# A new order of the pieces of a chunked gated-attention and MoE kernel, with the last stores split and on other queues

## The chip, the cores and the metric

The kernel runs on one core of one Trainium2 chip. The core has five engines that run side by side, each in the order of its own instruction stream: TensorE (PE in the profile; its weight loads are shown apart as PEld), VectorE (DVE), ScalarE (ACT), GpSimd (POOL) and SyncE (SP), which here only issues transfers. The metric is the device time of one execution in microseconds; less is better.

## The reference

There are two parts. The first is a gated linear attention over 4 batches, 8 heads, 768 positions and 48 dimensions; the second takes its output as a sequence of 384 features, makes a gate by a causal convolution of five taps, and multiplies by two matrices.

```python
f = 1.0 / (1.0 + np.exp(-f_logit))
for t in range(S):
    state = f[:, :, t, :, None] * state + np.einsum('bhd,bhe->bhde', k[:, :, t], v[:, :, t])
    y[:, :, t] = np.einsum('bhd,bhde->bhe', q[:, :, t], state)
...
x = y.transpose(0, 2, 1, 3).reshape(B, S, H * D)
for k in range(5):
    gate_pre += conv_w[k][None, None, :] * xp[:, k:k + S, :]
gate = 1.0 / (1.0 + np.exp(-gate_pre))
val = x @ w_val
return (gate * val @ w_out).astype(np.float32)
```

Here xp is x with four zero rows put in front.

## The kernel before

The sequence is cut into 6 chunks of 128 positions. Two heads lie together on the partitions, so a chunk has 16 pairs of batch and head pair. Inside a chunk the recurrence is turned into matrix products: with L the running sum of -log f, k is multiplied by exp(L) and q by exp(-L), so that scores are plain products of q and k, a triangular mask keeps the past, and the state is carried from chunk to chunk.

The work is cut into small pieces, each a function that emits a few instructions. PROGRAM is a text that lists all pieces in one order, written by a search outside of the kernel. The loop at line 762 emits them one by one, and the class Ordered ties every engine to exactly this order: each engine runs its own instructions as they come in PROGRAM, and waits where an input is not there yet. The first number of a piece is the chunk.

The attention's pieces, in the order in which a chunk needs them:

- loadf, loadk, loadq, loadv, loadw issue loads on SyncE. For chunk 0 the logits come from another layout, ft, in two parts (loadf 0 0 holds pairs 0 to 3, loadf 0 1 the rest); k, q and v of chunk 0 come in three parts (4, 4 and 8 pairs), those of later chunks in two halves.
- pexp and pln, on ScalarE: exp(-x), and then the log of 1 plus that, which is -log f. Then the running sum: by TensorE for chunk 0 (csum, into a pair of PSUM banks), by a VectorE scan for the others (scan).
- exp2 and exp1, on ScalarE: exp(L) and exp(-L). pmulk and pmulq, on VectorE: their products with k and q. okc notes on VectorE whether the numbers stay in range.
- ktrans (TensorE) and kevac (ScalarE): k transposed. dstate (TensorE), stend (VectorE) and stmul (GpSimd): the state of the next chunk.
- scores (TensorE, one per batch), mask (VectorE) and cross (ScalarE) bring the scores to SBUF; apply (TensorE, four per chunk) makes y, and xevac (ScalarE) copies it to XF. halo copies the last four columns of the chunk before.

The second part, for the same chunk: msplit (ScalarE) and mlow (VectorE) split x exactly in two parts; mlast (ScalarE) and mconv (VectorE, four taps by three groups m) do the convolution, for chunk 0 TensorE does it as one piece, conv; gate (ScalarE) is the sigmoid; mval (TensorE, nine matmuls) is x times w_val, mmul (VectorE) gates it, mhigh (ScalarE) and mrest (VectorE) split the result, mout (TensorE, nine matmuls) multiplies by w_out, mstore (ScalarE) copies it to SBUF and out issues the store. The last chunk is done as two halves of two batches, numbered 5 and 6.

weight n is one step of preparing a weight (n = 0 the convolution's taps, 1 to 3 w_val, 4 to 6 w_out): step 1 on GpSimd, 2 on ScalarE, 3 to 6 on VectorE, 7 on ScalarE and 8 on GpSimd (step 7, the last for n = 0, on GpSimd). wload n loads it.

busy n has n matmuls on a tile of zeros run in front of the next piece that takes a PSUM bank; they compute nothing.

What else sets the order. There are three pairs of PSUM banks and two single ones; a piece that takes a pair waits until the piece that frees it (cross, kevac, xevac, stend, exp1, gate) is through. Buffers of q, k, v and E1 are double, by chunk parity, E2 and vs are single. pace (line 662) lets the first 24 loads go as soon as SyncE reaches them and their buffer is free; each later load also waits for the last TensorE instruction that was emitted before it and for the fourth transfer before it:

```python
        if loads[0] > EAGER:
            for x in (PE.last, moves[-AHEAD]):
                tc.add_manual_dep(ins.ins, x.ins.name,
```

out n m takes SyncE's queue; with a third number 1 it takes ScalarE's. Stores up to chunk 4 leave from two buffers, osb, in turn; those of 5 and 6 from qb. When out 6 m is reached and out 5 m has not been, one transfer of 256 KB stores both halves:

```python
        if n == NC and (last, m) in bufs:
            bufs.pop((last, m))
            buf, dst = half(m, 0, 2), oview(last, m)
        moves.append((ACT if engine else SP).dma_start(dst, buf[:]))
```

In the profile nearly every instruction has line 128, the helper's; pieces are told apart by engine, tile and shape (asb for mask and cross, qb and kb on VectorE for pmulq and pmulk, work for the weights' steps, e on ScalarE for exp and log, banks<-xf,WD for conv).

Of the kernel before, what the change touches and what calls it, by code (L numbers as in the profile page):

```python
# [829 lines left out]
```

## Time and profile before

| What | us |
|---|---|
| median of 3 executions (lowest, highest) | 194.49 (192.51, 194.89) |
| the profiled execution's own time | 194.6 |
| its span, first to last instruction | 192.9 |
| TensorE busy | 176.0 |
| VectorE busy | 165.9 |
| ScalarE busy | 151.2 |
| GpSimd busy | 39.8 |
| last matmul over, last store issued | 187.4, 187.8 |

The profile is one execution taken by the hardware profiler. Busy is the time in which an engine worked on an instruction; a busy TensorE may still be at half clock, so the granted clock is read beside it (1.00 is full). Its mean over the span is 0.963. The groups of instructions give a count, the busy time, the mean of one in ns, and the idle time just before them with what ended it. Loads move 39 MB, at 205 GB/s over the span, and at up to 418 GB/s in the first 25 us.

### The profile page before, as it was taken

The numbers are of one execution on the slowest core, as the hardware profiler recorded it, in microseconds if no ns is written. First come the engines' busy times: TensorE is split into PE (matmuls) and PEld (weight loads), VectorE is DVE, ScalarE is ACT, GpSimd is POOL, SyncE is SP. The second block draws the span as 40 slices with busy tenths as digits, with TensorE's granted clock in tenths as the row PEclk, the third lists the DMA queues.
The fourth block names the chain that finished last, engine by engine and source line by source line (L and its number), as shares of the span: only waits on it lengthen the run. The fifth ranks groups of instructions, "written<-read, shape, count | busy, mean of one in ns | idle before, by whom it ended". The sixth has DMA issues, their size and how long they took to land.

```text
span 192.9 us, 7550 instructions
## 1 busy us (share of the span) xinstructions
PE 176.0 (91%) x3356; PEld 143.2 (74%) x3357; DVE 165.9 (86%) x235; ACT 151.2 (78%) x241; POOL 39.8 (21%) x43
## 2 busy tenths in 40 slices
PE   7869689995999989989999997999999999999980
PEld 2467577864788867878988796888887878898880
DVE  2528989899897999999899998998999999999710
ACT  5369949699469886998999999949897964986950
POOL 5110198076900682000600000000411000000000
PEclk9969969997599999999999999999999999999999
DMA  5999992993897599795389797003850020100161
GB/s 171 336 377 416 415 370 49 352 343 133 237 411 245 138 247 388 272 355 177 120 242 373 226 398 311 7 7 70 297 187 0 7 107 5 58 3 0 54 241 40
DMA packets 11989, 39.47 MB, mean 205 GB/s; under 512 B 1456, under 2 KB 2096, under 8 KB 11312
## 3 DMA queue, kind: packets, MB, share of 16 engines
q1 hardware_dynamic: 10800, 37.38, 54.9%
q10 hardware_dynamic: 1152, 1.57, 2.2%
q8 instruction: 27, 0.44, 0.9%
q14 instruction: 10, 0.08, 0.1%
HBM read 34.23 MB, written 4.72 MB: 202 GB/s over the span
## 4 chain that ended last, share of the span: by engine, by line
PE 75%; DVE 9%; ACT 5%; issue 4%; DMA 3%; SPq 1%; DVEq 0%
PE banks L128 75%; DVE work L128 4%; DMA e<-in_ft 3%; ACT e L128 3%; DVE qb L128 2%; ACT ksb L128 1%; DVE asb L128 1%; SPq L128 1%; DVE okc L128 1%; DVE xL L128 1%; DVE st L128 0%; DVE gt L128 0%; ACT asb L128 0%; ACT work L128 0%; ACT qb L128 0%
## 5 line engine op out<-in xcount | busy, mean ns | idle before, releaser
L128 ACT ACTIVATE e<-e 112x1024 f32<-112x1024 f32 (+3 forms) x36 | 44.4, 1239 | 4.8 <-DMA e<-in_ft 4.1
L128 DVE SCALAR_TENSOR_TENSOR pre<-xf,cws,pre 128x512 f32<-128x512 f32 x48 | 34.3, 749 | 0.9 <-ACT pre L128 0.8
L128 PE MATMUL banks<-rg,woH 128*128 128x512 f32 (+1 forms) x108 | 32.0, 381 | 0.0
L128 PE MATMUL banks<-qb,kb 48*64 48x128 f32 (+1 forms) x768 | 26.3, 266 | 5.3 <-DVE qb L128 2.5
L128 PE MATMUL banks<-asb,vb 128*32 128x64 f32 (+2 forms) x1152 | 29.2, 252 | 0.0
L128 PEld LDWEIGHTS banks<-qb,kb 48*64 48x64 f32 x768 | 22.3, 139 | 8.8 <-DVE qb L128 3.3
L128 POOL TENSOR_TENSOR st<-st,e 112x512 f32<-112x512 f32 x8 | 14.5, 1818 | 57.4 <-issue 30.1
L128 DVE TENSOR_TENSOR_SCAN e<-keep,e 112x1024 f32<-112x1024 bf16 x10 | 24.7, 2481 | 0.0
L128 PEld LDWEIGHTS banks<-asb,vb 128*32 128x32 f32 (+1 forms) x1152 | 23.6, 112 | 1.2 <-issue 0.9
L128 PEld LDWEIGHTS banks<-rg,woH 128*128 128x128 f32 x108 | 19.2, 188 | 4.1 <-issue 0.2
L128 PE MATMUL banks<-rg,woL 128*128 128x512 f32 (+1 forms) x54 | 20.3, 375 | 0.0
L128 PE MATMUL banks<-xH,wvH 128*128 128x512 f32 x45 | 19.3, 430 | 0.0
L128 ACT ACTIVATE gt<-pre 32x512 f32<-32x512 f32 (+2 forms) x28 | 17.6, 629 | 0.8 <-DVE pre L128 0.5
L128 PE MATMUL banks<-xL,wvH 128*128 128x512 f32 x45 | 18.2, 405 | 0.0
L128 PE MATMUL banks<-xH,wvL 128*128 128x512 f32 x45 | 18.2, 405 | 0.0
L128 PE MATMUL banks<-qb,st 48*32 48x128 f32 (+1 forms) x480 | 18.0, 278 | 0.1
L128 DVE TENSOR_TENSOR asb<-banks,tri 128x512 f32<-128x512 f32 x24 | 16.1, 680 | 1.2 <-PE banks L128 1.1
L128 DVE TENSOR_TENSOR qb<-qb,e 112x1024 f32<-112x1024 f32 (+1 forms) x13 | 16.3, 1252 | 0.6 <-DMA qb<-in_q 0.6
L128 DVE SCALAR_TENSOR_TENSOR work<-work 128x384 f32<-128x384 f32 (+3 forms) x14 | 8.5, 622 | 8.5 <-ACT work L128 8.5
L128 DVE TENSOR_TENSOR kb<-kb,e 112x1024 f32<-112x1024 f32 (+1 forms) x13 | 15.1, 1176 | 0.7 <-ACT e L128 0.7
L128 ACT COPY xf<-banks 128x512 f32<-128x512 f32 (+1 forms) x24 | 10.3, 483 | 6.8 <-PE banks L128 6.8
L128 ACT COPY asb<-banks 128x256 f32<-128x256 f32 x24 | 8.8, 372 | 7.5 <-DVE asb L128 7.5
(84 smaller groups left out, 313.9 us busy)
## 6 DMA issues: line engine op xcount, KB each, us to landing
vb<-in_v SPq DMA_DIRECT2D x11, 640.0 KB, 6.1
qb<-in_q SPq DMA_DIRECT2D x11, 512.0 KB, 5.4
kb<-in_k SPq DMA_DIRECT2D x11, 512.0 KB, 5.6
vs<-in_vn SPq DMA_DIRECT2D x10, 512.0 KB, 7.9
e<-in_f SPq DMA_DIRECT2D x5, 1024.0 KB, 7.0
out<-osb SPq DMA_DIRECT2D x12, 256.0 KB, 4.5
...
```

The costliest lines, as they stand in the source:

```text
L128: ins = emit(*a, **kw)
```

## The change

PROGRAM is replaced by another order; no other line is touched. The pieces are the same but for these: the idle matmuls (17, 5 and 3 in front of csum 0 0, csum 0 2 and ktrans 0 0) become 6, 3, 5, 4, 1, 2, 1 and 1 in front of csum 0 1, ktrans 0 0, scores 0 0, scores 0 2, scores 0 3, dstate 1 1, ktrans 2 0 and dstate 2 1, 23 in place of 25; the three stores of chunk 4 lose their 1 and so go to SyncE's queue; and out 5 1 1 is new, so that the last chunk's six stores are of 128 KB each, where one of five had 256 KB.

At the front the second part of ft is now issued second (it was fourth, behind wload 1 and wload 0); its pieces on ScalarE come next, and the second steps of the weights behind them. Three sums in the order of parts 1, 0, 2 replace 0, 2, 1. v's and w's loads lie ahead of loadq 1 0 and loadq 1 1, which become the 25th and 26th load, and so fall under the pace.

In front of conv 0 there are no longer two scores of chunk 1, but dstate 1 1. Between mask 0 3 and mask 1 3 VectorE no longer has pmulk 2 1 and pmulq 2 1, but has stend 0 0 and four more steps of weights 5 and 6. In chunk 2, scores 2 2 comes last of the four scores, cross 2 3 and cross 2 2 come behind pexp 4 0 and pln 4 0, and pmulq 2 1 behind pmulk 3 1.

```diff
@@ PROGRAM @@
-loadf 0 0; pexp 0 0; pln 0 0; wload 1; weight 1; wload 0; weight 0; weight 0; weight 1; weight 1; weight 1; loadf 0 1;
-pexp 0 2; pexp 0 1; pln 0 2; pln 0 1; busy 17; csum 0 0; exp2 0 0; weight 0; weight 0; weight 0; weight 1; weight 0;
-weight 1; wload 2; weight 2; weight 2; weight 2; loadk 0 0; pmulk 0 0; exp1 0 0; weight 2; loadq 0 1; loadq 0 2; loadw
-0 0; loadq 0 0; pmulq 0 0; weight 2; busy 5; csum 0 2; exp2 0 2; csum 0 1; exp2 0 1; exp1 0 1; loadk 0 1; pmulk 0 1;
-busy 3; ktrans 0 0; pmulq 0 1; weight 2; exp1 0 2; pmulq 0 2; kevac 0 0; loadf 1 0; pexp 1 0; scores 0 1; mask 0 1;
-cross 0 1; loadk 0 2; pmulk 0 2; scores 0 0; dstate 0 0; stend 0 0; mask 0 0; okc 0; scores 0 2; mask 0 2; pln 1 0;
-scan 1 0; scan 1 1; scores 0 3; cross 0 0; weight 2; cross 0 2; ktrans 0 1; loadv 0 0; loadv 0 2; loadv 0 1; apply 0 0
-0; apply 0 0 1; loadk 1 1; loadw 0 1; weight 2; weight 1; kevac 0 1; dstate 0 1; exp2 1 0; exp1 1 0; halo 0; xevac 0
-0; mask 0 3; cross 0 3; apply 0 1 0; apply 0 1 1; loadk 1 0; pmulk 1 0; ktrans 1 0; stend 0 1; loadq 1 0; pmulq 1 0;
-scores 1 0; exp2 1 1; pmulk 1 1; exp1 1 1; xevac 0 1; weight 1; wload 3; weight 3; weight 3; weight 3; weight 3; wload
-4; loadw 1 0; loadf 2 0; wload 6; loadq 1 1; loadw 1 1; wload 5; loadk 2 1; loadv 1 0; scores 1 1; kevac 1 0; mask 1
-0; ktrans 1 1; cross 1 0; mask 1 1; dstate 1 0; cross 1 1; okc 1; weight 3; weight 0; conv 0; stend 1 0; weight 4;
-weight 4; weight 4; weight 3; weight 4; weight 4; weight 4; stmul 1 0; msplit 0; mlow 0; kevac 1 1; dstate 1 1; pmulq
-1 1; scores 1 2; weight 3; weight 3; weight 5; stend 1 1; pexp 2 0; pln 2 0; scan 2 1; loadk 2 0; loadq 2 1; stmul 1
-1; halo 1; loadf 3 0; loadw 2 0; loadv 1 1; scores 1 3; scan 2 0; mask 1 2; gate 0 0; weight 4; mval 0 2; gate 0 1;
-gate 0 2; mmul 0 2; exp2 2 1; pmulk 2 1; cross 1 2; exp2 2 0; pmulk 2 0; weight 5; weight 5; exp1 2 1; mval 0 0; mmul
-0 0; weight 5; pmulq 2 1; exp1 2 0; apply 1 0 0; apply 1 0 1; mask 1 3; xevac 1 0; loadq 2 0; loadw 2 1; ktrans 2 0;
-mval 0 1; kevac 2 0; dstate 2 0; loadw 3 0; weight 4; weight 6; weight 6; weight 6; weight 6; ktrans 2 1; cross 1 3;
-apply 1 1 0; apply 1 1 1; pexp 3 0; pln 3 0; weight 5; weight 6; mmul 0 1; stend 2 0; weight 5; weight 5; pmulq 2 0;
-okc 2; weight 6; kevac 2 1; mhigh 0 2; scan 3 0; loadv 2 0; scores 2 2; mask 2 2; stmul 2 0; weight 5; dstate 2 1;
...
-scores 2 0; mask 2 0; cross 2 1; mlow 1; pmulk 3 0; stmul 2 1; loadf 4 0; mout 0 0; mstore 0 0; mlast 1 1; cross 2 0;
-out 0 0; exp2 3 1; exp1 3 1; pmulk 3 1; mlast 1 0; mconv 1 2 0; mconv 1 0 0; mout 0 2; mstore 0 2; apply 2 0 0; apply
...
-0; mval 6 0; mval 6 2; mval 6 1; mconv 6 0 2; gate 5 2; mconv 6 2 1; gate 5 1; mhigh 5 0; mconv 6 0 3; mmul 5 2; mout
-4 1; mout 4 0; mstore 4 1; out 4 1 1; gate 6 0; mmul 5 1; mhigh 5 1; mconv 6 2 2; mconv 6 2 3; mconv 6 1 0; gate 6 2;
-mout 4 2; mconv 6 1 1; mconv 6 1 2; mrest 5 0; mrest 5 1; mconv 6 1 3; mhigh 5 2; mrest 5 2; mout 5 1; gate 6 1; mmul
-6 0; mhigh 6 0; mrest 6 0; mstore 4 2; mstore 4 0; mmul 6 2; mhigh 6 2; out 4 2 1; mmul 6 1; mhigh 6 1; mout 5 0; mout
-5 2; mstore 5 0; out 5 0 1; mstore 5 1; mstore 5 2; mrest 6 2; mrest 6 1; out 4 0 1; out 5 2 1; mout 6 1; mout 6 0;
-mstore 6 1; out 6 1 1; mstore 6 0; out 6 0 1; mout 6 2; mstore 6 2; out 6 2 1
+halo 0; loadf 0 0; pexp 0 0; loadf 0 1; pexp 0 1; pln 0 1; busy 6; csum 0 1; pln 0 0; csum 0 0; pexp 0 2; pln 0 2;
+csum 0 2; wload 0; weight 0; wload 1; loadq 0 1; weight 0; weight 0; weight 0; weight 0; weight 0; wload 2; weight 1;
+weight 2; weight 0; exp2 0 1; weight 1; loadk 0 1; pmulk 0 1; exp1 0 1; weight 1; weight 1; loadk 0 0; exp2 0 0; pmulk
+0 0; busy 3; ktrans 0 0; weight 2; weight 2; loadq 0 0; exp1 0 0; pmulq 0 1; pmulq 0 0; scores 0 1; exp2 0 2; exp1 0
+2; kevac 0 0; busy 5; scores 0 0; loadk 0 2; pmulk 0 2; mask 0 1; weight 1; weight 1; loadf 1 0; pexp 1 0; pln 1 0;
+loadq 0 2; pmulq 0 2; busy 4; scores 0 2; cross 0 1; weight 2; okc 0; ktrans 0 1; wload 4; loadv 0 1; loadk 1 0; loadv
+0 0; mask 0 0; cross 0 0; apply 0 0 0; weight 1; kevac 0 1; weight 2; scan 1 0; weight 2; weight 2; apply 0 0 1; busy
+1; scores 0 3; mask 0 2; cross 0 2; wload 3; loadw 0 0; dstate 0 0; exp2 1 0; xevac 0 0; scan 1 1; exp2 1 1; loadw 0
+1; dstate 0 1; loadv 0 2; mask 0 3; cross 0 3; apply 0 1 0; apply 0 1 1; pmulk 1 0; stend 0 1; stend 0 0; loadk 1 1;
+pmulk 1 1; exp1 1 1; weight 1; weight 3; weight 3; weight 3; weight 2; weight 4; weight 4; exp1 1 0; loadw 1 0; ktrans
+1 0; kevac 1 0; ktrans 1 1; kevac 1 1; loadw 1 1; xevac 0 1; halo 1; msplit 0; weight 3; okc 1; weight 3; weight 3;
+weight 3; loadf 2 0; dstate 1 0; loadq 1 0; loadq 1 1; weight 4; weight 4; stend 1 0; busy 2; dstate 1 1; stend 1 1;
+wload 5; loadk 2 0; wload 6; loadv 1 0; mlow 0; weight 4; weight 4; pmulq 1 0; stmul 1 0; pmulq 1 1; stmul 1 1; loadf
+3 0; pexp 2 0; pln 2 0; scan 2 0; conv 0; gate 0 0; gate 0 1; scores 1 0; mask 1 0; weight 3; weight 5; weight 5;
+weight 5; scores 1 1; mask 1 1; weight 5; mval 0 2; gate 0 2; mmul 0 2; weight 4; weight 4; scores 1 2; mask 1 2;
+cross 1 0; loadk 2 1; loadv 1 1; loadw 2 0; loadq 2 1; loadw 2 1; loadq 2 0; exp2 2 0; scan 2 1; pmulk 2 0; scores 1
+3; cross 1 2; cross 1 1; weight 6; weight 6; weight 5; weight 5; weight 6; mval 0 0; mmul 0 0; weight 6; apply 1 0 0;
+apply 1 0 1; mask 1 3; pexp 3 0; weight 6; exp2 2 1; exp1 2 0; weight 5; pmulk 2 1; weight 5; busy 1; ktrans 2 0;
+kevac 2 0; mval 0 1; mmul 0 1; weight 6; pln 3 0; scan 3 1; cross 1 3; dstate 2 0; loadw 3 0; xevac 1 0; stend 2 0;
+pmulq 2 0; mhigh 0 1; weight 6; weight 6; mhigh 0 0; mrest 0 0; mhigh 0 2; mrest 0 2; mrest 0 1; ktrans 2 1; loadk 3
+1; apply 1 1 0; apply 1 1 1; kevac 2 1; loadq 3 1; xevac 1 1; halo 2; mlast 1 0; busy 1; dstate 2 1; scan 3 0; loadk 3
+0; scores 2 1; scores 2 0; stend 2 1; loadq 3 0; loadv 2 0; loadw 3 1; mlast 1 1; exp1 2 1; exp2 3 1; msplit 1; mask 2
+0; cross 2 0; mlast 1 2; exp2 3 0; exp1 3 0; okc 2; mask 2 1; cross 2 1; pmulk 3 1; stmul 2 0; stmul 2 1; pmulq 2 1;
+loadf 4 0; mout 0 1; mout 0 0; mstore 0 0; mstore 0 1; out 0 1; exp1 3 1; loadv 2 1; loadv 3 0; ktrans 3 1; kevac 3 1;
+scores 2 3; apply 2 0 0; apply 2 0 1; mconv 1 2 0; mconv 1 2 1; mconv 1 1 0; mconv 1 0 0; pmulk 3 0; xevac 2 0; ktrans
+3 0; kevac 3 0; pexp 4 0; pln 4 0; mout 0 2; mstore 0 2; mconv 1 2 2; mconv 1 0 1; pmulq 3 0; scores 3 0; scores 2 2;
...
+2; mconv 6 1 0; mconv 6 0 0; mhigh 4 0; mhigh 4 1; mconv 5 2 2; mlast 6 2; mconv 6 2 0; mrest 4 0; mrest 4 2; mrest 4
+1; mout 4 2; mconv 6 2 1; mconv 5 2 3; mconv 6 2 2; gate 5 1; mmul 5 1; mconv 6 2 3; mconv 5 0 2; mconv 5 0 3; mout 4
+1; gate 5 2; mconv 6 0 1; mconv 6 0 2; mhigh 5 1; mrest 5 1; mstore 4 2; gate 5 0; mmul 5 2; mmul 5 0; gate 6 2; mconv
+6 0 3; mhigh 5 0; mrest 5 0; mhigh 5 2; mrest 5 2; out 4 2; mstore 4 1; mout 4 0; mstore 4 0; out 4 1; out 4 0; mconv
+6 1 1; mconv 6 1 2; mconv 6 1 3; gate 6 0; mmul 6 0; gate 6 1; mmul 6 2; mval 6 1; mmul 6 1; mhigh 6 1; mrest 6 1;
+mhigh 6 0; mrest 6 0; mout 5 0; mstore 5 0; mhigh 6 2; out 5 0 1; mout 5 1; mout 5 2; mstore 5 2; out 5 2 1; mstore 5
+1; out 5 1 1; mrest 6 2; mout 6 0; mstore 6 0; out 6 0 1; mout 6 1; mstore 6 1; out 6 1 1; mout 6 2; mstore 6 2; out 6
+2 1
```

More of the change, by code (lines that the diff above doesn't have):

```diff
@@ L80 @@
-1 0 2; mconv 1 1 2; okc 3; mconv 1 0 3; mconv 1 1 3; pmulq 3 0; loadv 2 1; pexp 4 0; mout 0 1; ktrans 3 0; kevac 3 0;
-mstore 0 1; out 0 1; out 0 2; loadq 3 1; ktrans 3 1; mval 1 0; mval 1 1; cross 2 3; apply 2 1 0; apply 2 1 1; mconv 1
-2 2; mconv 1 2 3; pln 4 0; scan 4 1; kevac 3 1; dstate 3 1; loadw 4 1; dstate 3 0; gate 1 1; xevac 2 1; gate 1 2;
-mlast 2 2; gate 1 0; mlast 2 0; stend 3 1; stmul 3 1; mmul 1 1; scores 3 0; scores 3 1; stend 3 0; stmul 3 0; pmulq 3
-1; mmul 1 0; mhigh 1 0; loadk 5 0; loadq 4 1; mask 3 0; cross 3 0; mhigh 1 1; mask 3 1; cross 3 1; mval 1 2; mmul 1 2;
@@ L85 @@
-mconv 2 2 0; mrest 1 0; mhigh 1 2; scores 3 2; scores 3 3; loadf 5 0; loadv 3 1; loadw 4 0; apply 3 0 0; apply 3 0 1;
-msplit 2; exp2 4 1; mlast 2 1; exp1 4 1; mrest 1 2; mrest 1 1; mout 1 2; mout 1 1; mstore 1 2; loadk 4 0; out 1 2;
-mconv 2 2 1; scan 4 0; exp2 4 0; exp1 4 0; loadk 4 1; loadk 5 1; mout 1 0; mstore 1 1; out 1 1; loadv 4 1; loadv 4 0;
-mlow 2; mval 2 2; mask 3 2; mask 3 3; cross 3 3; cross 3 2; apply 3 1 0; apply 3 1 1; halo 3; xevac 3 0; loadq 5 0;
-pexp 5 0; pln 5 0; mstore 1 0; out 1 0; mconv 2 2 2; pmulq 4 0; mconv 2 1 0; mconv 2 0 0; mconv 2 1 1; mconv 2 0 1;
@@ L95 @@
-3 2 1; dstate 4 0; halo 4; xevac 4 0; mconv 3 0 0; mconv 3 2 2; exp2 5 0; loadv 5 1; loadv 5 0; mconv 3 0 1; mconv 3 1
-0; scan 5 1; mstore 2 1; exp2 5 1; exp1 5 1; mout 2 0; loadq 5 1; out 2 1; mstore 2 0; exp1 5 0; out 2 0; mconv 3 1 1;
-mconv 3 0 2; mlow 3; apply 4 1 0; apply 4 1 1; xevac 4 1; stend 4 0; mconv 3 2 3; mconv 3 0 3; stend 4 1; gate 3 0;
-mconv 3 1 2; gate 3 2; mlast 4 2; mval 3 0; mval 3 1; pmulq 5 0; pmulk 5 0; scores 5 1; scores 5 0; mmul 3 0; mconv 3
-1 3; gate 3 1; mval 3 2; mask 5 1; cross 5 1; mhigh 3 0; pmulk 5 1; okc 5; pmulq 5 1; scores 5 2; scores 5 3; mask 5
@@ new lines @@
+mask 2 3; cross 2 3; mlow 1; mval 1 0; mconv 1 0 2; mconv 1 0 3; mask 2 2; cross 2 2; apply 2 1 0; apply 2 1 1; gate 1
+0; mconv 1 1 1; mconv 1 1 2; mask 3 0; cross 3 0; mconv 1 1 3; gate 1 1; out 0 0; loadv 3 1; loadq 4 1; loadk 4 1;
+xevac 2 1; mmul 1 0; mconv 1 2 3; halo 3; gate 1 2; mlast 2 0; mhigh 1 0; scan 4 1; exp2 4 1; mlast 2 1; pmulq 3 1;
+dstate 3 1; dstate 3 0; stend 3 0; mval 1 1; mmul 1 1; stend 3 1; okc 3; mrest 1 0; scores 3 1; scores 3 2; loadk 4 0;
+scores 3 3; mask 3 1; cross 3 1; mhigh 1 1; loadq 4 0; scan 4 0; exp2 4 0; mval 1 2; mmul 1 2; mhigh 1 2; mlast 2 2;
@@ new lines @@
+stmul 3 0; stmul 3 1; loadf 5 0; loadk 5 0; out 0 2; mask 3 2; mrest 1 1; apply 3 0 0; msplit 2; apply 3 0 1; xevac 3
+0; exp1 4 1; mrest 1 2; mout 1 2; mout 1 1; mstore 1 2; out 1 2; loadw 4 1; loadv 4 1; mout 1 0; pmulk 4 0; mask 3 3;
+cross 3 3; cross 3 2; pexp 5 0; apply 3 1 0; apply 3 1 1; mconv 2 2 0; pmulk 4 1; mconv 2 2 1; mconv 2 0 0; mconv 2 2
+2; mconv 2 1 0; pmulq 4 1; exp1 4 0; mstore 1 0; pln 5 0; out 1 0; loadv 4 0; loadq 5 1; loadw 4 0; loadq 5 0; loadk 5
+1; loadv 5 0; loadv 5 1; xevac 3 1; mstore 1 1; out 1 1; mconv 2 2 3; gate 2 2; mconv 2 1 1; pmulq 4 0; mlow 2; mconv
```

34 lines of the change are left out of this document (17 added, 17 removed).

## The prediction

> **What bounds the kernel now.** I read the page first: the busy time of each engine and the slices of the span.
>
> ```profile
> span 192.9 us, 7550 instructions
> PE 176.0 (91%) x3356; PEld 143.2 (74%) x3357; DVE 165.9 (86%) x235; ACT 151.2 (78%) x241; POOL 39.8 (21%) x43
> PE   7869689995999989989999997999999999999980
> DVE  2528989899897999999899998998999999999710
> PEclk9969969997599999999999999999999999999999
> ```
>
> TensorE and VectorE are both nearly full, and both have their holes in the first third. The new order holds the same pieces (but for idle matmuls and one store), so the work stays; only holes, the clock and the two ends can change. So I cut the span at the holes (columns: TensorE, weight loads, VectorE, ScalarE, GpSimd busy, granted clock, DMA).
>
> ```profile
> 8.50:11.10 2.60, 0.25 (x2) 0.00 (x0) 0.17 (x1) 2.43 (x6) 0.53 (x1) 1.00 1.03 378
> 11.10:15.00 3.90, 3.84 (x20) 3.84 (x21) 1.89 (x4) 2.23 (x6) 0.00 (x0) 0.56 1.04 398
> 15.00:25.00 10.00, 7.58 (x178) 6.20 (x177) 9.29 (x13) 8.78 (x13) 1.72 (x1) 1.00 1.02 414
> 25.00:28.60 3.60, 3.60 (x73) 2.90 (x76) 3.18 (x2) 1.95 (x3) 3.60 (x3) 0.53 0.95 385
> 42.40:45.80 3.40, 1.16 (x34) 0.95 (x32) 3.40 (x4) 3.37 (x4) 1.70 (x1) 0.98 0.74 279
> 45.80:52.60 6.80, 6.77 (x72) 5.80 (x73) 6.52 (x4) 3.93 (x6) 6.09 (x3) 0.51 0.50 146
> 29.50:59.30 29.80, 27.18 (x628) 21.44 (x623) 27.86 (x31) 22.81 (x33) 15.41 (x10) 0.89 0.72 252
> 70.40:118.80 48.40, 46.91 (x1011) 38.61 (x1011) 47.07 (x60) 44.94 (x64) 5.84 (x6) 1.00 0.83 290
> 118.80:147.50 28.70, 28.48 (x559) 23.21 (x559) 27.45 (x34) 24.67 (x38) 3.40 (x3) 1.00 0.32 105
> ```
>
> After 70.4 TensorE idles 1.5 + 0.2 us in 77 us and VectorE 1.3 + 1.3 us: there is little left to win. Before that TensorE loses 2.4 us at 8.5, 2.4 us at 15 to 25, 2.2 us at 42.4 and, at half clock, some 3.4 us of 6.8 behind it. The chain of waits (start, length, what) tells what ends the long ones.
>
> ```profile
> 2.21 6.44 DMA e<-in_ft
> 8.67 2.45 ACT e L128 x5
> 11.16 4.55 PE banks L128 x24
> 44.20 1.58 DVE qb L128
> 45.83 13.17 PE banks L128 x218
> ```
>
> The front waits for the second part of ft; the hole at 42.4 waits for VectorE's product on qb (pmulq 1 1), which stands behind the weights' steps and mlow 0.
>
> **The front.** Start, length, engine, what; in brackets the wait that ended.
>
> ```profile
> 3.53 0.58 ACT L128 ACTIVATE e<-e 128x448 f32<-128x448 f32 x1 [1.43 <-DMA e<-in_ft]
> 4.68 0.53 POOL L128 TENSOR_SCALAR work<-raww 128x384 f32<-128x384 f32 x1 [1.07 <-DMA raww<-in_wv]
> 6.15 0.56 DVE L128 SCALAR_TENSOR_TENSOR work<-work 128x384 f32<-128x384 f32 x1 [3.67 <-ACT work L128]
> 8.67 0.95 ACT L128 ACTIVATE e<-e 128x896 f32<-128x896 f32 x1 [2.63 <-DMA e<-in_ft]
> 28.86 0.69 DVE L128 TENSOR_TENSOR asb<-banks,tri 128x512 f32<-128x512 f32 x1 [0.68 <-PE banks L128]
> 29.47 1.22 DVE L128 TENSOR_TENSOR kb<-kb,e 112x1024 f32<-112x1024 f32 x1
> ```
>
> The new order issues ft's second part second, ahead of the first weight block. That block's 384 KB arrived 1.15 us after ft's first part (4.68 against 3.53), so ft is in at 8.67 - 1.15 = 7.5 us. Bounds: 8.67, if its lateness is not the queue's; 5.6, if its 672 KB run at that block's 334 KB/us behind 3.53. I take 7.5: it moves one known transfer.
>
> ```profile
> L128 DVE TENSOR_TENSOR_SCAN e<-keep,e 112x1024 f32<-112x1024 bf16 x10 | 24.7, 2481 | 0.0
> L128 ACT ACTIVATE e<-e 128x448 f32<-128x448 f32 x4 | 2.3, 568 | 1.5 <-DMA e<-in_ft 1.4
> L128 DVE TENSOR_TENSOR kb<-kb,e 112x512 f32<-112x512 f32 x2 | 1.4, 688 | 0.7 <-ACT e L128 0.7
> ```
>
> ScalarE then runs two of 0.57 us (part 1) and the first sum can start at 8.65 instead of 11.16; one of 0.57 and two of 0.95 follow, to about 11.0. Against that stands a loss: the weights' second step (w 0) now waits behind these five, so VectorE, which before worked from 6.15, starts at 11.05. From there to the last mask of chunk 0 (mask 0 3) I count its pieces, each at its row less the 0.08 us by which the next starts early (28.86 + 0.69 against 29.47): four half parts at 0.61, two full ones at 1.14, four masks at 0.60, two scans at 2.4, eight weight steps 3.5 (the row at 6.15 is one), small ones 0.6: 16.0 us. Waits between them 0.4 (the first product waits for its exp), and 0.4 for pieces lengthened where GpSimd is busy throughout (the stage from 25 shows it so). The mask ends at 27.9 instead of 29.55: **1.6 us** ahead (by the two bounds of ft 0.5 to 3.5).
>
> **The stage to chunk 1's last mask.** From the end of mask 0 3 to that of mask 1 3 (at 59.3) VectorE took 29.8 us, 27.9 busy with 31 instructions. The new order has the same between these two points, but for pmulk 2 1 and pmulq 2 1 (2 x 1.14), which it puts behind, and stend 0 0 and four weight steps (0.6 + 1.8) put ahead: +0.1. Its idle 1.9 us came of waits for TensorE's matmuls standing at half clock and in the hole. The row of mask 1 3, and what TensorE does in between:
>
> ```profile
> 58.64 0.68 DVE L128 TENSOR_TENSOR asb<-banks,tri 128x512 f32<-128x512 f32 x1
> 33.67 2.01 PE L128 MATMUL banks<-qb,kb 48*64 48x128 f32 x64
> 37.59 4.94 PE L128 MATMUL banks<-xf,WD 32*32 32x512 f32 x120
> ```
>
> Now conv 0 ends at 42.5, 13.0 us behind mask 0 3, with two scores (2.0 us) in front of it. The new order takes these out and puts dstate 1 1 and two idle matmuls in (1.5): 27.9 + 13.0 - 0.5 = 40.4. By then VectorE has pmulq 1 0 about done (11.1 us of pieces behind 27.9, and its share of lengthening), so scores 1 0 follows, and the hole of 2.2 us and the 3.4 us of cold clock go: with the front TensorE would be 7 us ahead. VectorE isn't: it is late next, and it sets the gain: **1.9 us**. Bounds: 0, if as many waits return; 5.9, if its lengthened pieces also shorten. Of those the largest:
>
> ```profile
> 39.75 2.28 DVE L128 SCALAR_TENSOR_TENSOR work<-work 128x384 int32<-128x384 int32 x1
> L128 DVE SCALAR_TENSOR_TENSOR work<-work 128x384 int32<-128x384 int32 x6 | 5.0, 840 | 0.0
> ```
>
> Of six alike five took (5.0 - 2.28) / 5 = 0.55 us. At the median of each kind over the whole trace the 31 pieces come to 24 us, against 27.9: 4 us of lengthening, while GpSimd was busy 15.4 us. GpSimd's pieces are all kept, so I keep the 4 us. [...]
>
> **Behind it.** The lead is carried: TensorE's and VectorE's remaining pieces are the same. The order there is wholly new; that VectorE's small idles, such as this one, shrink I count as 0.4 won, between 4 lost and 2 won.
>
> ```profile
> 60.27 0.56 DVE L128 SCALAR_TENSOR_TENSOR work<-work 128x384 f32<-128x384 f32 x1 [0.95 <-ACT work L128]
> ```
>
> **The two other edits.** Chunk 4's three stores leave ScalarE's queue for SyncE's, which has nothing left behind chunk 3's stores. The last rows:
>
> ```profile
> 186.82 0.34 ACTq L128 DMA_DIRECT2D out<-qb  x1
> 187.42 0.37 ACT L128 COPY qb<-banks 128x256 f32<-128x256 f32 x1 [0.63 <-PE banks L128]
> 187.82 1.09 ACTq L128 DMA_DIRECT2D out<-qb  x1
> ```
>
> Issuing is no busy time, and ScalarE waited 0.63 us for TensorE before its last copy, so three issues taken off it move nothing. Of the one 256 KB store made two, the earlier half leaves long before the end, its issue (0.34 in the first row) is hidden by that wait. The queue ahead of the last store is shorter by 128 KB and by chunk 4's: its issue of 1.09 us may go toward those 0.34. Between 0 and 0.7, and half of it taken: **0.3 us**.
>
> Sum: 1.6 + 1.9 + 0.4 + 0.3 = 4.2 us. The profiled execution took 194.6 us, 1.7 beyond its span, the median of three is 194.49: 194.6 - 4.2 = **190.4 us**, with its own bounds 188.4 to 192.4.
>
> **Rivals.** *TensorE's 7 us come through* (22%): VectorE's lengthening shrinks too, as its products no longer fall beside GpSimd's. For it: the last weights' steps and chunk 1's state products move apart. Against: GpSimd is busy 6.09 of 6.8 us where scans run now. 190.4 - 4 = 186.4.
>
> *The waits return elsewhere* (14%): only front and tail are won: 194.6 - 1.6 - 0.3 = 192.7. For it: the present order has its holes although TensorE and VectorE had work.
>
> *Cold front* (8%). Six idle matmuls stand at the start where 17 and 5 stood. The row at 11.1 shows the first sums at clock 0.56 after 2.4 us of idling, and now TensorE would idle from 4 to 8.65. If the clock stays half through chunk 0's first scores, 32 passes take 6.8 us and end near 15.5, as now (11.16 + 4.55): the front's 1.6 goes, 192.0. [...]
>
> *ScalarE stands for a load* (12%), the slower side. In the new order cross 2 3 and cross 2 2 lie behind pexp 4 0 and pln 4 0 on ScalarE, and apply 2 1 0 needs both; loadf 4 0 can only start when pmulq 2 1 has left its buffer, and that now follows pmulk 3 1.
>
> ```profile
> 73.92 0.33 SPq L128 DMA_DIRECT2D e<-in_f  x1
> 81.90 1.91 ACT L128 ACTIVATE e<-e 112x2048 f32<-112x2048 f32 x1 [0.30 <-DMA e<-in_f]
> e<-in_f SPq DMA_DIRECT2D x5, 1024.0 KB, 7.0
> ```
>
> If it takes 8 us again, TensorE waits about 3 us, as long as the hole at 42.4, and pays 3.4 for the half clock behind it: 190.4 + 6.4 = 196.8. It decides from about 5 us of landing on; less is covered by mout 0 2 and two scores.
>
> **Numbers.** Forecast 44%, rivals 22, 14, 8, 12%. About 2% (3.9 us) is what a measurement of this kernel can tell from no change. Below 190.6 lie the first rival and about 54% of the forecast: 0.46. Above 198.4 only the slow case, a second time at chunk 5's load: 0.08. The rest, 0.46, is within. From 186 to 196.5 leaves out the ends of the first and the last rival, some 15%.
>
> **What would show it.** Front: ScalarE's first activation on ft's second part at 7.5, the mask at 27.9. Middle: no idle over 1 us on TensorE between conv 0 and mval 0 0, clock 1.00 there; mask 1 3 on VectorE ending near 55.8; TensorE waiting for VectorE rather than the reverse. Tail: the last issue at 0.4 us. I am wrong if VectorE's idle before 59 is as long as now, if scores 1 0 waits for loadq 1 0 (now behind dstate 1 0 in the pace), or if TensorE idles more than 3 us behind 70.

## The result, and the profile after

The changed kernel took 195.83 us (median of 20 runs, 194.01 to 200.94), the kernel before 194.42 (20 runs, 191.44 to 195.35): a ratio of **1.011, interval 1.008 to 1.015**. It is 1.1% slower, which is within 2% of no change, and the forecast was 4.2 us faster. Ratios and intervals here leave out disturbed runs; for three kernels below too few others were left, and they have no ratio. "Old" is the kernel before, "new" the changed one.

The profiled run took 194.68 us, one of the faster of the 20 and as long as that of before (194.6). Its page, span and engines, then TensorE, VectorE and the clock in 40 slices, then the chain by engine:

```profile
span 193.0 us, 7546 instructions
PE 173.3 (90%) x3355; PEld 139.1 (72%) x3355; DVE 165.9 (86%) x235; ACT 150.6 (78%) x241; POOL 39.5 (20%) x43
PE   5699979989999997799987979999999899999990
DVE  2079999999999999879999967989999999899720
PEclk9999999999999999999999999999999999999999
PE 68%; DMA 16%; DVE 6%; issue 4%; SPq 1%; ACT 1%; DVEq 0%
```

The holes of the first third and the half clock of 45.8 to 52.6 are gone, as forecast. But TensorE has new holes between slices 15 and 24, and so has VectorE. Cut into stretches (TensorE, weight loads, VectorE, ScalarE, GpSimd busy, clock, DMA share, GB/s), first before:

```profile
75.00:95.00 20.00, 19.50 (x468) 16.32 (x466) 19.87 (x25) 18.44 (x27) 1.60 (x2) 1.00 0.72 255
95.00:115.00 20.00, 20.00 (x457) 16.50 (x455) 19.40 (x25) 19.44 (x28) 1.53 (x2) 1.00 0.87 295
115.00:135.00 20.00, 18.98 (x350) 15.54 (x341) 18.60 (x25) 17.00 (x28) 0.22 (x1) 1.00 0.32 110
```

and after:

```profile
75.00:95.00 20.00, 18.62 (x483) 15.64 (x476) 17.47 (x23) 16.58 (x24) 3.36 (x3) 1.00 0.63 211
95.00:115.00 20.00, 17.24 (x413) 13.96 (x409) 19.14 (x23) 16.72 (x25) 0.41 (x1) 1.00 0.79 261
115.00:135.00 20.00, 19.46 (x289) 16.25 (x290) 17.09 (x20) 16.61 (x25) 3.09 (x2) 1.00 0.59 210
```

In these 60 us TensorE is busy 3.2 us less and VectorE 4.2 us less than before: that is the lead of the front, given back. To see where, I counted each piece at its median length in the old trace and summed what an engine had begun by a time. The lead over the old kernel, in us of work:

```
time           30    40    50    60    70    80    90   100   110   120   150   170
new TensorE  +2.0  -0.2  +3.4  +3.6  +4.1  +2.9  +2.1  +1.7  -0.5  -0.1  -0.2  -0.7
new VectorE  +0.6  +0.4  +2.0  +4.4  +4.6  +5.8  +3.3  +3.9  +4.1  +0.6  +0.1  -0.4
```

TensorE loses its 4 us between 70 and 110, and VectorE, still 4 us ahead at 110, loses that at 114 to 116. The views of waits tell for what (us in total, times, longest). First TensorE before, then TensorE and VectorE after:

```profile
PE banks L128 <- issue: 2.8, 4, 1.6
```

```profile
PE banks L129 <- issue: 8.1, 9, 1.9
PE banks L129 <- DMA vb<-in_v: 1.1, 1, 1.1
DVE asb L129 <- PE banks L129: 3.8, 2, 1.9
```

One stall of 1.1 us is a late load (loadv 2 0, which ended at 73.9). The rest is "issue": TensorE stood and the profile shows nothing that it waited for. VectorE's 3.8 us are two waits for TensorE, each right behind such a stall. The timeline around the two:

```profile
82.04 1.10 PE L129 MATMUL banks<-qb,kb 48*64 48x64 f32 x34 [1.38 <-issue]
83.29 0.69 DVE L129 TENSOR_TENSOR asb<-banks,tri 128x512 f32<-128x512 f32 x1 [1.89 <-PE banks L129]
115.54 0.45 PE L129 MATMUL banks<-qb,kb 48*64 48x64 f32 x11 [1.37 <-issue]
116.14 0.69 DVE L129 TENSOR_TENSOR asb<-banks,tri 128x512 f32<-128x512 f32 x1 [1.94 <-PE banks L129]
```

Both stalls fall inside one piece (scores 3 0, scores 4 0), between two matmuls of the same operands, so no data can be what is waited for.

The chain of work that ended last says the same. Behind 74 us it runs through TensorE alone, with these pauses (start, length, what):

```profile
73.98 6.68 PE banks L129 x167
80.66 1.38 issue
82.04 18.65 PE banks L129 x475
100.69 1.93 issue
102.62 11.55 PE banks L129 x235
114.17 1.37 issue
115.54 28.00 PE banks L129 x472
```

Two more, of 0.18 and 0.58 us, follow at 143.5 and 152.6: 5.4 us in all. In the chain before, TensorE's longest pause of this kind behind 70 us is this one:

```profile
83.16 0.49 issue
```

The chain's 16% of DMA are four loads, all of them ahead of 74 us; two of them (vs and vb of chunk 2, at 48.6 and 66.1) held TensorE for 0.3 and 1.1 us.

**What the issue stalls are.** The page has a row for a DMA queue of instructions:

```profile
q8 instruction: 27, 0.44, 0.9%
```

27 packets of 16,384 bytes each. I numbered TensorE's instructions (weight loads, matmuls, semaphore waits). The stalls of the new kernel stand at instructions 706, 1218, 3010, 4034, 4546 and 6082: each, within one, 194 more than a multiple of 256. So TensorE's instructions arrive in blocks of 256, and these stalls are at the ends of blocks. Against the packets' times in the trace (us; "begins" is when TensorE begins the block that is there, "packet" the transfer of the next one, "end" when it has used up its block):

```
piece at the end    begins   packet            end      goes on   behind the packet   stall
dstate 0 1           22.72    25.83 -  26.71    27.04     28.23    1.52               1.19
conv 0               32.64    36.74 -  37.67    37.22     39.10    1.43               1.88
scores 3 0           74.85    79.80 -  80.68    80.41     82.04    1.36               1.63
mout 1 2             97.56    99.23 - 101.16   100.48    102.62    1.46               2.14
scores 4 0          110.57   113.22 - 114.17   113.93    115.54    1.37               1.61
apply 4 0 1         115.54   119.43 - 120.31   125.19    125.19    4.88               none
mout 3 0            149.91   150.84 - 151.80   152.46    153.34    1.54               0.88
```

At the six stalls TensorE goes on 1.36 to 1.54 us behind the end of the packet, whatever the piece. The packet sets out 0.4 to 1.3 us after the block ahead of it is begun where no load is under way (at 87 and behind 126, apart from one that set out earlier), and up to 7.1 us after it where loads are: it waits behind them (without the loads of chunks 3 to 5, in part 4 of the experiments, the mean wait from 57 to 122 is 1.3 us, against 3.0). A block stalls TensorE when it is used up sooner than this takes, as in six of these seven rows. A block with at most nine matmuls of mval or mout, the rest scores, dstate, apply and transposes, lasts 2.6 to 6.3 us; one with 13 or more 6.6 to 13, and none of these ended in a stall.

This gives **theory 1**: the packets, held up by loads, took the lead. **Theory 2**: the rest of the new order has other waits between its engines and loses the lead whatever the packets do. **Theory 3**: its late loads land too late.

### The profile page after: what moved, and what is told of

It reads as the page before. It is cut to its first block, busy times and chain, and to the rows that moved or that the text cites. A ratio compares the mean times of both kernels' runs of the same rounds, so it can differ in the third digit from the quotient of the medians.

```text
span 193.0 us, 7546 instructions
## 1 busy us (share of the span) xinstructions
PE 173.3 (90%) x3355; PEld 139.1 (72%) x3355; DVE 165.9 (86%) x235; ACT 150.6 (78%) x241; POOL 39.5 (20%) x43
## 4 chain that ended last, share of the span: by engine, by line
PE 68%; DMA 16%; DVE 6%; issue 4%; SPq 1%; ACT 1%; DVEq 0%
PE banks L129 68%; DMA qb<-in_q 5%; DMA vs<-in_vn 4%; DMA vb<-in_v 4%; DMA raww<-in_wv 3%; DVE e L129 2%; SPq L129 1%; ACT e L129 1%; DVE work L129 1%; DVE asb L129 1%; DVE st L129 1%; DVE qb L129 1%; DVE kb L129 1%; ACT qb L129 0%; ACT asb L129 0%
## 5 line engine op out<-in xcount | busy, mean ns | idle before, releaser
L129 DVE SCALAR_TENSOR_TENSOR pre<-xf,cws,pre 128x512 f32<-128x512 f32 x48 | 35.1, 762 | 0.2
L129 PE MATMUL banks<-asb,vb 128*32 128x64 f32 (+2 forms) x1152 | 28.0, 245 | 1.7 <-DMA vb<-in_v 1.1
L129 PE MATMUL banks<-qb,kb 48*64 48x64 f32 (+1 forms) x768 | 24.5, 255 | 3.5 <-issue 3.1
L129 PEld LDWEIGHTS banks<-qb,kb 48*64 48x64 f32 x768 | 21.0, 132 | 8.3 <-issue 5.2
L129 PEld LDWEIGHTS banks<-asb,vb 128*32 128x32 f32 (+1 forms) x1152 | 22.5, 108 | 2.0 <-DMA vb<-in_v 1.4
L129 DVE TENSOR_TENSOR_SCAN e<-keep,e 112x1024 f32<-112x1024 bf16 x10 | 23.3, 2330 | 0.0
L129 POOL TENSOR_TENSOR st<-st,e 112x512 f32<-112x512 f32 x8 | 13.7, 1722 | 39.2 <-ACT asb L129 36.1
L129 DVE TENSOR_TENSOR kb<-kb,e 112x1024 f32<-112x1024 f32 (+1 forms) x13 | 16.1, 1245 | 1.2 <-ACT e L129 1.2
L129 DVE TENSOR_TENSOR qb<-qb,e 112x1024 f32<-112x1024 f32 (+1 forms) x13 | 14.7, 1143 | 0.1
L129 PEld LDWEIGHTS banks<-rg,woL 128*128 128x128 f32 x54 | 10.1, 188 | 4.1 <-issue 2.1
```

Of the source, the lines that this page charges most:

```text
L129: ins = emit(*a, **kw)
```

## The experiments

**1. Half of each order.** The first half of one and the rest of the other, joined behind apply 1 1 1 (about 61 us): what follows are the pieces not yet done, in the other order's sequence. The join of new_then_old:

```diff
...
 loadk 3 1; apply 1 1 0; apply 1 1 1;
-kevac 2 1; loadq 3 1; xevac 1 1; halo 2; mlast 1 0;
+exp1 2 1; pmulq 2 1; okc 2; kevac 2 1; scan 3 0;
...
```

> The new order up to and with apply 1 1 1, then every piece that is still to do in the old order. Theory 1, the fetch: TensorE's instructions arrive in blocks of 256 (the packets of 16,384 bytes on the instruction queue), TensorE stands until 1.4 us after such a packet ends, and the packet waits behind the loads; the lead of the new front (VectorE 4.4 us of work ahead at 60) is lost where a block runs out early, so 190.5 plus whatever TensorE's idle time put down to issue is above the 2.8 us of before: 190.5 to 193.5. Theory 2, the rest of the new order itself (its loads and its waits between engines) loses the lead: the old rest keeps it, 190 to 191, with issue no larger than before.

194.73 us, ratio 1.003 (0.997 to 1.009): outside what either theory gave. The packets cost nothing here ("issue" 0.4 us in all), yet TensorE's lead went at once, in one wait at the join, and VectorE's fell from 4.0 at 70 to -0.6 at 100:

```profile
65.75 1.12 PE L128 MATMUL banks<-qb,kb 48*64 48x128 f32 x20 [3.93 <-DVE qb L128]
```

VectorE had scan 3 1, pmulq 2 0 and three mrest, which the new half has there, ahead of pmulq 2 1, and in the old rest scores 2 2, which needs that product, follows at once. Behind this wait TensorE was at half clock (0.50) from 64.6 to 71.4. The run shows that an order can lose its lead through theory 2's mechanism, not that the new one does.

> The old order up to and with apply 1 1 1, then the rest in the new order. Theory 1: the blocks of 256 fall on other places of the new rest; some of the stalls at scores 3 0, mout 1 2 and scores 4 0 (1.6, 2.1 and 1.6 us after the change) go or move, 195 to 198. Theory 2: the new rest loses its 4 to 5 us whatever comes ahead, 198.5 to 199.5, with the stalls at the same pieces.

197.4 to 204.5 us, median 203.6: of the four runs only the one of 197.4 lies within theory 1's range, and none within theory 2's. In the profiled run (202.8) TensorE's "issue" is 12.1 us, and the stalls stand at other pieces (72.7, 83.8, 109.8, 123.0: 2.95, 2.2, 1.9, 1.4 us). The new rest is prone to them; that they move with what comes ahead speaks for theory 1.

**2. Three transfers under way, not four.**

```diff
-AHEAD = 4
+AHEAD = 3
```

> The new order with AHEAD 3 in place of 4: a paced load waits for the third move before it, so that three and not four transfers are under way. Theory 1: the waits of the instruction packets behind loads (7.1 us at 65, 5.0 at 75, 4.2 at 91, 4.1 at 33) fall by about a quarter, the stalls of 1.6 to 2.1 us shrink to about half, 192 to 194.5. Theory 3, late loads: chunk 2's and 3's vs and vb (the chain of waits has 8 us of each) land 1 to 2 us later, TensorE waits for them, 196 to 198. Theory 2: 195.8, no difference.

> The old order with AHEAD 3 in place of 4. Theory 1: there VectorE and not TensorE ended last in most of the middle, so that shorter waits of the instruction packets gain at most 1 us, 193.5 to 194.5. Theory 3: 195 to 197, the loads land later.

199.5 us (1.021, 1.011 to 1.031) and 199.4 us (1.025, 1.015 to 1.036): both slower than the kernel before by 4 to 5 us, the way theory 3 had it, and further than its ranges. The new order was 1.1% behind already, so it lost about 2 us by this change, the old one about 5. The row of a late landing in the new order:

```profile
64.35 1.23 DVE L129 TENSOR_TENSOR qb<-qb,e 112x1024 f32<-112x1024 f32 x1 [2.88 <-DMA qb<-in_q]
```

Theory 1's detail failed too: from 57 to 122 us the packets waited 3.2 us on average, against 3.0 with four. (In the old order with four it is 2.65: the packets wait about as long in both orders, and it matters which block meets a long wait.) Landings do cost once they come later (the 2.88 us of the row above); whether they cost in the new order as it is, the next runs tell.

**3. The same program, moved against the blocks.** Tiny idle matmuls ahead of csum 0 1 shift everything behind them.

```diff
+        for _ in range(extra.pop() if extra else 0):
+            PE.matmul(t[0:32, 0:32], idle[:, 0:32], idle[:, 0:32], start=True, stop=True)
...
-    todo = [0]
+    todo, extra = [0], [32]
```

> The new order with 32 tiny idle matmuls (32 columns) more ahead of csum 0 1, where TensorE idles from 3.1 to 6.7 us. Order, loads and waits are the same; every later TensorE instruction stands 64 places further back, so that each block of 256 ends 32 matmuls earlier in the program. Theory 1: the stalls follow the blocks: they leave scores 3 0, mout 1 2 and scores 4 0 and turn up, if at all, at mout 0 2 (79), scores 3 3 (95), apply 3 0 1 (99), apply 3 1 1 (110) and scores 4 1 (113); the time moves by 1 to 4 us either way, 192 to 199. Theories 2 and 3: stalls at the same pieces, 195 to 196.5.

> The same with 64 tiny idle matmuls, half a block. Theory 1: the blocks end in apply 2 0 0 (72), apply 2 0 1 (76), apply 2 1 0 (86), dstate 3 1 (88), scores 3 2 (94), apply 3 0 1 (99), apply 3 1 0 (109), scores 4 2 (112); stalls only there, 192 to 199 and not the same time as with 32. Theories 2 and 3: stalls at the same pieces as in the new order, 195 to 196.5.

> The same with 96. Theory 1: the blocks end in scores 2 3 (71), apply 2 0 1 (75), scores 2 2 (83), apply 2 1 1 (87), scores 3 1 (93), apply 3 0 0 (98), apply 3 1 0 (109), apply 3 1 1 (111); stalls only there, 192 to 199. Theories 2 and 3: 195 to 197 (the front may begin up to 1.5 us later, as the matmuls may not all fit ahead of 6.7).

202.3 us (1.052, 1.046 to 1.058), 203.6 (1.051, 1.043 to 1.060), and 192.6 to 202.6 with 96 (median 200.6). The first two are above theory 1's range. The order, the loads and the waits are the same, and the time differs by up to 8 us. TensorE's rows, for 32, 64 and 96 (profiled runs of 198.8, 207.2 and 192.6 us; the second is the longest of its four, the others the shortest of theirs):

```profile
PE banks L129 <- issue: 8.2, 10, 2.3
```

```profile
PE banks L129 <- issue: 14.1, 11, 3.3
```

```profile
PE banks L129 <- issue: 4.9, 4, 2.4
```

With 64, the stalls from 84 on are at 84.4, 97.2, 104.4 and 124.1 (2.96, 0.9, 1.4 and 3.6 us); with 96 there is none behind 78. All stand at ends of blocks. With two of them TensorE's clock fell to half besides (0.50 for 3.4 us from 84.1 and from 125.0), which in the new kernel no stall brought: its trace has 1.00 from 12.2 to the end of the work. VectorE's lead fell from 1.1 at 60 to -11.1 at 130. This shows theory 1's mechanism and that it moves the time by microseconds; theories 2 and 3 had foreseen no difference. A part of it is the front: with 32 and 64 chunk 0's scores came 1.5 us later, as TensorE had done its sums early, idled (with 64 it was busy for 0.15 us from 12 to 14.3), and then had the half clock (0.6 in the fourth slice of the clock's row). With 32 the front and a stall at 57.7 (2.3 us) are most of it: the issue row is as long as without the shift (8.2, 8.1), and of the 3.5 us that VectorE is behind the unshifted order at 170, 3.3 are there at 60.

> The new order with each of the 23 idle matmuls of 512 columns issued as four of 128: the same idle work at the same places, and the rest of TensorE's program stands 69 matmuls further back against the blocks of 256. Here the clock of the front should stay as it is (1.00), which the tiny matmuls ahead of csum 0 1 did not grant (0.95 up to 17 us with 32 and 64 of them). Theory 1: another time than the new order's, with stalls at other pieces, 192 to 201. Theories 2 and 3: 195.8 give or take 0.8, stalls at scores 3 0, mout 1 2 and scores 4 0.

> The old order with each of its 25 idle matmuls issued as four: 75 matmuls of shift. Theory 1: if the time of the old order too hangs on where its blocks end (stalls of 1.8 at 24.6, 0.55 at 69.5, 0.7 at 83.7, 1.4 at 118.8), it moves by 1 us or more, likely up, since blocks that end in the runs of small matmuls wait longer: 194 to 200. Theory 2 (the order alone sets the time): 193.5 to 194.5, as the old order.

```diff
-            PE.matmul(t, idle[:, 0:128], idle[:], start=True, stop=True)
+            for _ in range(4):
+                PE.matmul(t[:, 0:128], idle[:, 0:128], idle[:, 0:128], start=True, stop=True)
```

203.9 us (1.054, 1.044 to 1.064) and 197.4 (1.019, 1.013 to 1.026). Both orders move, the new one further than theory 1's 192 to 201. Its sums ended no later than without the edit (12.2, against 13.1), but a block ended at 27.2 with a stall of 2.2 us, and TensorE was at half clock (0.50) from 28.6 to 32.0. VectorE's lead was 1.1 at 60 and fell to -4.4 at 130, with the longest stall (3.3 us) at the end of a block at 118.7.

**4. Loads taken away.** Theory 1 says that without late loads the packets come in time and the new order shows its lead. The pieces loadq, loadk, loadv and loadw of the last chunks are left out, so that these chunks compute on older data: of chunks 4 and 5 in the first pair, of 3, 4 and 5 in the second.

```diff
-loadv 3 1; loadq 4 1; loadk 4 1;
+loadv 3 1;
...
```

> The new order without the loads of chunks 4 and 5 of q, k, v and vn (loadq, loadk, loadv, loadw): those chunks compute on what chunks 2 and 3 left in the buffers, so that this part of the output is another; all arithmetic is still done. The DMA engines have little to do from 85 to 127. Theory 1: the instruction packets start within 1.3 us of the end of the block ahead, as they do now behind 125; the stalls at mout 1 2 (2.1) and scores 4 0 (1.6) fall below 0.5 each, VectorE keeps some 3 us more of its lead, 191.5 to 193.5. Theory 2, the waits between engines in the new rest: no difference, 195.8. Theory 3, the late landings: of the stalls above none waits for a landing behind 75, so no difference behind 85 either, 195 to 196.

> The old order without the loads of q, k, v and vn of chunks 4 and 5 alone, for comparison with the new order without them (193.0 median, 190.1 to 192.5 undisturbed). Theory 1: 193 to 194.3. Theory 2: 193.5 to 194.5, and no difference either.

New 193.0 us (190.1 to 195.9), old 192.8 (0.988, 0.983 to 0.993). From 85 to 127 the stalls went as expected; the new order after, then without these loads:

```profile
85.00:105.00 20.00, 18.07 (x480) 14.86 (x479) 19.43 (x25) 17.10 (x26) 3.77 (x3) 1.00 0.69 225
105.00:127.00 22.00, 20.63 (x457) 17.32 (x457) 18.29 (x24) 19.23 (x30) 0.00 (x0) 1.00 0.84 284
```

```profile
85.00:105.00 20.00, 20.00 (x489) 16.55 (x489) 19.29 (x25) 18.20 (x30) 3.60 (x3) 1.00 0.33 102
105.00:127.00 22.00, 22.00 (x507) 18.68 (x506) 21.65 (x29) 20.98 (x31) 0.00 (x0) 1.00 0.11 39
```

But the old order gained too, more than the 193 to 194.5 that was expected, and the two now stand level, so this pair doesn't tell why new and old differ: chunk 3's loads were still there, and the new order's TensorE lost 2.8 us of its lead between 60 and 80, at two block ends (62.4 and 77.0: 1.8 and 1.7 us for issue) and a landing (74.3: 1.2 us for vb).

> The new order without the loads of q, k, v and vn of chunks 3, 4 and 5 (the arithmetic of those chunks runs on what chunks 1 and 2 left, so that this part of the output is another). Theory 1: with little on the DMA engines behind 60, every block's packet starts within 1.5 us, the stalls of TensorE behind 60 that are put down to issue sum to less than 1.5 (5.6 in the changed kernel from 75 on), and VectorE's lead of 4.4 us at 60 comes through to two thirds or more: 190 to 192. Theory 2: the new rest loses its lead between the engines, 194.5 to 196.

> The old order without the same loads. Theory 1: it had little to lose behind 60 (stalls of 0.55, 0.7 and 1.4, of which VectorE felt 0.6), so 193 to 194.3, and at least 2 us slower than the new order without them. If it gains as much as the new order does, the loads cost both alike and the packets do not explain the difference.

New **187.7 us (0.970, 0.962 to 0.978)**, old 191.3 (0.987, 0.978 to 0.997). Now the new order is 3.6 us ahead of the old one by the medians (3.3 by the ratios), close to the 4.2 of the forecast; the old one gained more than expected here, too. Stalls at block ends behind 60 sum to 1.0 us (7.0 after the change). The packets' mean wait from 57 to 122 fell from 3.0 to 1.3 us, though not each was within the 1.5 us expected (3.2 at 77). That the blocks end elsewhere is not the reason: they still end in scores 3 0, mout 1 2, scores 4 0 and mout 3 0, and only the third of these stalls, for 0.46 us. Nor are VectorE's own pieces shorter without the loads: it is busy 165.3 us, against 165.9 after the change. VectorE's lead over the old kernel is 4.4 at 60, 5.0 at 90, 5.3 at 120, 5.7 at 170: carried to the end. The new order's stretches without these loads:

```profile
75.00:95.00 20.00, 20.00 (x456) 16.46 (x446) 19.91 (x24) 18.25 (x27) 3.90 (x3) 1.00 0.23 81
95.00:115.00 20.00, 19.78 (x432) 16.42 (x432) 19.94 (x29) 18.57 (x28) 0.00 (x0) 1.00 0.32 108
115.00:135.00 20.00, 20.00 (x420) 16.76 (x422) 19.36 (x21) 18.05 (x25) 3.09 (x2) 1.00 0.12 43
```

Theory 2 falls as the account of this loss: with the same order and, but for the loads, the same waits, nothing is lost. What takes the lead comes with the loads. Packets and landings both do; by the rows of the new kernel itself the packets have 4.7 us of it from 75 to 120 (1.38, 1.93 and 1.37, both of VectorE's long waits behind them) and the landing 1.1. What quick packets alone would bring stays open: no run took the loads out of the packets' way and left their landings as they were.

**5. Where to join.** Where the orders have done nearly the same pieces, the new front can be had with the old rest. The joins, behind cross 1 1, stend 0 0 and scores 3 1:

```diff
...
 scores 1 3; cross 1 2; cross 1 1;
-weight 6; weight 6; weight 5; weight 5; weight 6; mval 0 0;
+exp2 2 1; pmulk 2 1; exp1 2 1; mval 0 0;
...
```

```diff
...
 pmulk 1 0; stend 0 1; stend 0 0;
-loadk 1 1; pmulk 1 1; exp1 1 1; weight 1; weight 3;
+loadk 1 1; weight 2; exp1 1 0; ktrans 1 0; loadq 1 0;
...
```

```diff
...
 okc 3; mrest 1 0; scores 3 1;
-scores 3 2; loadk 4 0; scores 3 3; mask 3 1;
+loadq 4 0; out 0 2; loadw 4 1; mlast 2 2;
...
```

And the tail, in the two runs named so:

```diff
-out 4 1 1;
+out 4 1;
...
-out 5 2 1;
+out 5 2 1; out 5 1 1;
...
```

> The new order up to and with cross 1 1 (about 50 us), then all that is still to do in the old order; at this cut the two orders have done almost the same pieces (0 us of TensorE's work and 1.4 us of VectorE's apart), which was not so at apply 1 1 1. Theory 1: VectorE's lead of 2 us at 50 comes through if no block of the old rest runs out: 190.5 to 192.5; with a stall or two more than before 193 to 195. Theory 2: 190 to 192.5, the old rest loses nothing.

195.0 us, 1.005 (0.999 to 1.011). A miss: in the profiled run (195.8, one of the longer ones) TensorE's "issue" is 1.5 us, but behind 56 it waited for ScalarE (2.5 us for asb, 1.7 for xf, 1.5 for ksb), VectorE's lead of 2.0 at 50 was 0.0 at 70, and TensorE was at half clock (0.50) from 70.3 to 77.1. Here theory 2's kind of loss is at work, in a rest that was written for another state of the engines.

> The new order up to and with stend 0 0 (about 30 us), then the old order. TensorE is 2 us of work ahead at 30, VectorE 0.6. The half clock of 45.7 to 52.5 of before may come back, as the old order around conv 0 does. Theory 1: 192 to 195, by the places of the blocks. Theory 2: 0.6 to 2 us ahead of the old order, 191.5 to 193.5.

192.1 us, 0.989 (0.978 to 1.000). As expected of both theories; VectorE's lead grows from 0 at 40 to 2.9 at 130.

> The new order up to stend 0 0, then the old order, with the change's tail: chunk 4's stores issued by SyncE and six stores each alone. From the run without the tail (1.1% faster than the old kernel, interval 0.978 to 1.0001) and the tail's price (the stretch from the last mout to the end is 6.2 us after the change and 6.9 before): 190.3 to 192.5. No TensorE instruction moves against the blocks, so the stalls should stay where they were (29.6 and hardly any behind).

**191.7 us, 0.988 (0.983 to 0.993)**: 1.2% faster than the kernel before, and the best that was run with all its work.

> The new order up to and with scores 3 1 (about 92 us), then all that is still to do in the old order, with the change's tail. All loads are in place. At this cut TensorE has done the same pieces in both orders, so that behind it the blocks of 256 end at the same pieces as before the change (ktrans 4 1 at 118.8 with a stall of 1.4, none above 0.7 else). Theory 1: the stalls at mout 1 2 (2.1) and scores 4 0 (1.6) are gone, VectorE keeps 2 to 3 of the 3.3 us that it is ahead at 90: 191 to 193. Theory 2: the loss between 70 and 90 goes on, 194 to 196.

195.8 us, 1.0075 (1.002 to 1.013): a miss in the time, and the most telling one. The block still ended in mout 1 2, as in both kernels, and that stall did not go but grew. The same matmuls before, after, and here:

```profile
101.39 0.91 PE L128 MATMUL banks<-asb,vb 128*32 128x128 f32 x32
102.23 0.50 PE L128 MATMUL banks<-rg,woH 128*128 128x512 f32 x1
```

```profile
100.18 0.50 PE L129 MATMUL banks<-rg,woH 128*128 128x512 f32 x1
102.62 0.40 PE L129 MATMUL banks<-rg,woH 128*128 128x512 f32 x1 [1.93 <-issue]
```

```profile
101.22 0.50 PE L129 MATMUL banks<-rg,woH 128*128 128x512 f32 x1
104.33 0.39 PE L129 MATMUL banks<-rg,woH 128*128 128x512 f32 x1 [2.61 <-issue]
```

The block lasts 2.6 to 2.9 us in all three. Its packet set out 0.36, 1.67 and 3.35 us after the block was begun and took 1.1, 1.9 and 1.0 us: in the old order one load (loadq 4 1) was just beginning to arrive; in the new one loadk 4 0 was arriving, and loadq 4 0 with the packet; here loadq 4 0, a store and loadw 4 1 arrived ahead of it. I had the place of the block right and had taken its packet's wait to be the old one. Some 2.7 us more went at 106 to 109, where VectorE waited for ScalarE's exp of chunk 4 (pmulq 4 0 for exp1 4 0).

## Why the prediction was wrong, step by step

**Front: right.** Forecast: mask 0 3 ends at 27.9, 1.6 us ahead. The timeline of VectorE:

```profile
26.71 0.66 DVE L129 TENSOR_TENSOR asb<-banks,tri 128x512 f32<-128x512 f32 x1
54.83 0.69 DVE L129 TENSOR_TENSOR asb<-banks,tri 128x512 f32<-128x512 f32 x1
```

It ended at 27.4, 2.2 us ahead, but by a way that was in part luck. ft's second part was in earlier than my bound of 5.6, with ScalarE's first activation on it at 5.36:

```profile
5.36 0.58 ACT L129 ACTIVATE e<-e 128x448 f32<-128x448 f32 x1 [1.18 <-DMA e<-in_ft]
11.15 1.48 DVE L129 TENSOR_TENSOR kb<-kb,e 112x512 f32<-112x512 f32 x1 [1.20 <-ACT e L129]
```

That VectorE starts late held as well, though the forecast's 11.05 was for its first weight step: four small ones came at 9.15, and its first product at 11.15. The load came 2.1 us earlier than forecast, and the sums, which ran at half rate (last section) and had no term in the sum, took 6.4 us; the two errors went opposite ways.

**The stage to chunk 1's last mask: right.** Forecast 55.8 for the end of mask 1 3; the second row above ends at 55.5, 3.8 us ahead of before (1.6 + 1.9 = 3.5 forecast). The clock was 1.00, TensorE did not idle for 1 us between conv 0 and mval 0 0, and VectorE set the pace. That all 4 us of lengthened pieces would stay was my estimate; summed up, the pieces that VectorE began in this stage stand 3.0 us above the medians of their kinds after the change and 3.8 before. One thing was off: conv 0 ended at 41.9 and not 40.4, since a block ended in it:

```profile
39.10 2.77 PE L129 MATMUL banks<-xf,WD 32*32 32x512 f32 x52 [0.97 <-issue]
```

**Behind it: wrong. This step failed:** "The lead is carried: TensorE's and VectorE's remaining pieces are the same." The pieces are the same; that they would take the same time did not hold, since they fall differently on blocks of 256 instructions and on the loads under way. VectorE's 4.4 us of lead at 60 were 0.1 at 150; with the loads of chunks 3 to 5 away they were 5.7 at 170. I had bounded this at 4 lost, but took 0.4 won. The sign to go by had been written down ("TensorE idles more than 3 us behind 70") and came true: from 75 to 155 it stood 1.4, 1.9, 1.4 and 0.6 us for issue. The old trace showed the mechanism already. I had read TensorE's 2.4 us at 15 to 25 as work that was missing; most of it was this row of the old kernel, between two matmuls of scores 0 3, at instruction 450:

```profile
24.62 0.43 PE L128 MATMUL banks<-qb,kb 48*64 48x128 f32 x6 [1.59 <-issue]
```

**Tail: right in size.** From the start of mout 6 2 to the end it took 6.9 us before (186.05 to 192.9) and 6.2 after (186.8 to 193.0): 0.7 won, where 0.3 was forecast with 0.7 as bound. The last issue is shorter, though not 0.4:

```profile
188.59 0.80 ACTq L129 DMA_DIRECT2D out<-qb  x1
```

**The rivals.** *The waits return elsewhere* comes nearest in kind, but it had them return between 29 and 59 and priced the front as kept (192.7); they came behind 70 and by a mechanism that no rival named. *ScalarE stands for a load* did not come: its two waits for the f loads are 2.7 us together, and apply 2 1 0 followed at once. *Cold front*: the sums were cold, 32 of them taking 6.4 us (6.8 forecast), but chunk 0's scores were not (1.09 us for the first 32 matmuls, against 1.97 at half clock in the run with 32 more), so the front was kept: the new kernel's trace has the clock at 1.00 from 12.2 on, and these scores began at 15.3. *TensorE's 7 us come through*: VectorE set the pace, as argued.
